# Retention followed by a PReLU feed-forward block: the order of 3802 operations written out in the source instead of found by a list scheduler

## The chip, the cores and the metric

The kernel runs on one core of one Trainium2 chip. The metric is the device time of one execution in microseconds (us). Five engines take part, each working through its own queue in order: TensorE (PE, with PEld for the loading of weights), VectorE (DVE), ScalarE (ACT), GpSimd (POOL) and SyncE (SP), which here issues the DMA transfers.

## The reference

Everything is float32. The first part is retention without softmax, for 8 batches and 8 heads of 576 positions by 64; the second is a feed-forward block on 4608 tokens.

```python
scores = scale * np.matmul(q, k.transpose(0, 1, 3, 2))
Dmat = np.where(rel >= 0, gamma[:, None, None] ** rel[None, :, :], 0.0)
attn = np.matmul(scores * Dmat, v)                 # (8, 8, 576, 64)
x = attn.transpose(0, 2, 1, 3).reshape(4608, 512)
h = x @ w_in                                       # w_in 512 x 2048
g = np.maximum(h, 0.0) + alpha * np.minimum(h, 0.0)
out = g @ w_out                                    # w_out 2048 x 512
```

## The kernel before, in words

Retention is computed in chunks of 64 positions: inside a chunk as masked scores times values, between chunks through a running state (the sums of key times value, decayed from chunk to chunk). The first two batches go in six parts with all heads at once (`load_part`, `part_scale`, `part_transposes`, `part_scores`, `part_states`, `part_values`, `last_part`). The other batches go by pairs of heads in `joint`: per pair one group of score and state products (L920, L923, with one of L913) and two groups of value products (L861). All of these are small matmuls of 64 or 128 rows.

The feed-forward block takes blocks of 256 tokens against an eighth of w_in (256 columns, a "unit") and the matching rows of w_out. While the first two batches run, eight units are computed with plain float32 matmuls (`unit_plain`, L1091; `second_plain`, L1122). All others are computed with operands split into three pieces of float32r, in 128x512 matmuls: h in `unit_roll` (L1188) and `unit_two` (L1222), the second product in `second` (L1340). The pieces of g, of x and of the weights are made by ACT, DVE and POOL (`split_g` L1260 to L1267, `split_roll` L1158 to L1163, `split_w` L783 to L787); w_in and w_out arrive as 64-bit words and are first turned into float32 by two ACT, three DVE and one POOL operation each (`convert`, L730 to L754). At the start and behind the first part, matmuls of the identity whose result nobody reads keep PE occupied (`fill`, L1405).

Every operation is first recorded by `do` (engine, cost, function that issues it, what it reads and writes), in the order of the source, and numbered from 0 to 3801. Nothing is issued then. Afterwards `dues` and `plan` (L229 to L336) order the list: `dues` goes backwards from the end and gives each operation a due time, `plan` goes forwards with constants for an engine's latency, the wire of the DMAs and the loading of instructions and takes the most urgent ready operation. After 12 rounds of that, 243 random changes of the due times in windows of 40 us are tried and kept where the planned total does not get longer. The last loop (L1709 onwards) issues the operations in the planned order. Two things are decided in that loop beside the order in each queue:

- Operations marked `lock` (664 of those of DVE and POOL) never run on both engines at once: where one follows a locked one of the other engine in the order, it waits for it (the dependency with the reason "port").
- In the first 100 us of the plan a DMA issued by SP waits until no more than 5 x 256 KB lie ahead of it (the dependency with the reason "bytes in flight", L211 to L219).

Some lines to which the prediction refers: L455 scales queries or values of a part on POOL, L479 transposes with PE, L485 copies the transposes out with ACT, L503 scores, L510 their mask on DVE, L526 states, L541 their sums on DVE, L574 and L599 values, L588 a copy of two numbers on ACT ("spy") for which the second half of the values waits, L631 the copies of the result into x, L1097 the ReLU of a plain unit.

Of the kernel before, what the change touches and what calls it, by code (L numbers as in the profile page):

```python
# [21 lines left out]
def kernel(  # L22
# [96 lines left out]
    for i in range(NBIT - 1):  # L119
# [8 lines left out]
                            op=ALU.mult)  # L128
# [24 lines left out]
    ops, land = [], [LAND[0]]  # L153
# [65 lines left out]
                flight.append((ins, size))  # L219
        do(eng, 0.56, f, r, w, late=size / rate, hold=hold)  # L220

    flight, now = [], [0.0]
    LIMITED, IN_FLIGHT = 100.0, 5 << 18

    LAT = {"PE": 0.2}

    users = []

    def wait(d, op):  # L229
        return d.land if d.late else 0.0 if d.eng == op.eng else LAT.get(d.eng, 0.1)  # L230

    def dues(after):
        users[:] = [[] for _ in ops]
        for op in ops:
            for d in op.deps:
                users[d.n].append(op)
        due = [0.0] * len(ops)
        left = [len(users[op.n]) for op in ops]
        can = [0.0] * len(ops)
        free = {e: 0.0 for e in BEGIN}  # L240
        ready = {e: [] for e in BEGIN}
        for op in ops:
            if not left[op.n]:
                ready[op.eng].append(op)
        for _ in ops:
            pick = None
            for e, queue in ready.items():
                if queue:
                    t0 = min(max(free[e], can[op.n]) for op in queue)
                    op = max((op for op in queue if max(free[e], can[op.n]) <= t0 + 0.02),  # L250
                             key=lambda op: after[op.n])
                    t = max(free[e], can[op.n])
                    if pick is None or t < pick[0]:
                        pick = t, op
            t, op = pick
            ready[op.eng].remove(op)
            free[op.eng] = t + op.cost
            due[op.n] = -(t + op.cost)
            for d in op.deps:
                left[d.n] -= 1  # L260
                can[d.n] = max(can[d.n], t + op.cost + wait(d, op) + d.late)
                if not left[d.n]:
                    ready[d.eng].append(d)
        return due

    def plan(due):
        last = -min(due)
        left = [len(op.deps) for op in ops]
        ready = {e: [] for e in BEGIN}
        rest = [op.n for op in ops if op.eng == "PE"]  # L270
        end, begin, order = [0.0] * len(ops), [0.0] * len(ops), []
        free, held, port, wire, kinds = dict(BEGIN), {}, [0.0, ""], 0.0, {e: e for e in BEGIN}
        can = [0.0] * len(ops)

        at = [CHUNK - 190, 0.0]
        for op in ops:
            if not op.deps:
                ready[op.eng].append(op)

        def earliest(op):  # L280
            t = max(free[op.eng], can[op.n], op.hold)
            for b in op.banks:
                if b in held:
                    t = max(t, max([x + LAT.get(e, 0.1) for e, x in held[b].items()
                                    if e != op.eng] or [0.0]))
            if op.lock and port[1] != op.eng:
                t = max(t, port[0])
            if op.late:
                t = max(t, wire - BACKLOG, due[op.n] + last - HOLD)
            if op.size and at[0] + op.size > CHUNK:  # L290
                t = max(t, at[1] - op.cost * (CHUNK - at[0]) / op.size)
            return t + SWITCH.get(op.eng, 0.0) * (kinds[op.eng] != op.kind)

        while len(order) < len(ops):
            pick = None
            for e, queue in ready.items():
                if not queue:
                    continue
                c = [(earliest(op), op) for op in queue
                     if e != "PE" or op.n <= rest[0] + AHEAD_PE]  # L300
                if not c:
                    continue
                t0 = min(t for t, _ in c)
                t, op = min((x for x in c if x[0] <= t0 + SLACK.get(e, 0.05)),
                            key=lambda x: (due[x[1].n], x[1].n))
                if pick is None or t < pick[0]:
                    pick = t, op
            t, op = pick
            ready[op.eng].remove(op)
            if op.eng == "PE":  # L310
                rest.remove(op.n)
            begin[op.n] = t
            kinds[op.eng] = op.kind
            free[op.eng] = end[op.n] = t + op.cost
            if op.size:
                at[0] += op.size
                if at[0] >= CHUNK:
                    at[0] -= CHUNK
                    over = end[op.n] - op.cost * at[0] / op.size
                    at[1] = over + FETCH + min(max(wire - over, 0.0), 0.8)  # L320
            if op.late:
                wire = max(wire, t + op.cost) + op.late
                end[op.n] = wire
            for b in op.banks:
                held.setdefault(b, {})[op.eng] = t + op.cost
            if op.lock:
                if port[1] == op.eng or t + op.cost > port[0]:
                    port[:] = [t + op.cost, op.eng]
            order.append(op)
            for u in users[op.n]:  # L330
                left[u.n] -= 1
                can[u.n] = max(can[u.n], end[op.n] + wait(op, u))
                if not left[u.n]:
                    ready[u.eng].append(u)
        total = max(end)
        return total, order, begin, end  # L336

    AHEAD_PE = 150
    WINDOWS, STRETCH, TRIES, ROUNDS = 27, 20.0, 9, 9
    CHUNK, FETCH = 256, 3.1  # L340
    BACKLOG, HOLD = 2.0, 30.0
    LAG, HOLD_X = 2, 100.0
    X_TWO, QUICK, NQUICK, WDVE = 12, 13, 2, 16
    PUMP_R = ((1, 1), (1, 1))
    EARLY, JOINTS = 1, {(s, i): 1 for s in range(14) for i in range(2) if (s, i) not in ((0, 0), (8, 1), (10, 1), (13, 0), (13, 1))}
    PUMP0, PUMP = ((1, 2), (0, 1), (0, 1), (0, 1)), ((1, 2), (1, 2), (0, 1), (0, 1))
    GROUPS = (("v0",), ("v1",), ("x", "su"))
    SLACK, SWITCH = {"PE": 0.2}, {"PE": 0.1}
    BEGIN = {"PE": 1.9, "ACT": 0.5, "DVE": 5.5, "POOL": 5.4, "SP": 0.5}


    def slot(pool, tag, shape, dtype=FP32, bank=False):
        return Slot(tag, lambda: pool.tile(shape, dtype, tag=tag, name=f"{tag}_{next(serial)}"),
                    bank)
# [619 lines left out]
    order = [(kb, (2, 3, 0, 1) if kb % 2 and kb > 1 else (0, 1, 2, 3)) for kb in range(NKB - 2)]  # L974
# [599 lines left out]
    queue = []  # L1574
# [24 lines left out]
    free = [0, 1, 2, 3, 4]  # L1599
# [20 lines left out]
    last = singles - 1  # L1620
    t = 8
    for s in range(last):
        some = [visits[kb] for kb in (1 + s, 2 + s) if 2 <= kb <= last]
# [63 lines left out]
    second_last(*queue)  # L1687


    due = dues([op.n for op in ops])  # L1690
    best = made = plan(due)
    for _ in range(12):
        again = dues(made[3])
        made = plan(again)
        if made[0] < best[0]:
            best, due = made, again
    rng = np.random.RandomState(1)
    for n in range(ROUNDS * WINDOWS):
        lo = STRETCH * (n // TRIES % WINDOWS)
        some = [i for i, t in enumerate(best[2]) if lo <= t < lo + 2 * STRETCH]  # L1700
        other = list(due)
        for i, x in zip(some, rng.uniform(-1, 1, len(some)) * (1.0, 3.0, 9.0)[n % 3]):
            other[i] += x
        made = plan(other)
        if made[0] <= best[0]:
            best, due = made, other

    port = None
    for op in best[1]:  # L1709
        now[0] = best[2][op.n]  # L1710
        ins = op.fn()
        if op.lock:
            if port and port[0] != op.eng:
                tc.add_manual_dep(ins.ins, port[1].ins.name, mybir.DependencyInfo(
                    mybir.DependencyClass.Sync, mybir.DependencyReason.DATA), reason="port")
            port = op.eng, ins
# [31 lines left out]
```

## Time and profile before

| what | value |
|---|---|
| runs | 923.28, 919.66, 919.31 us; median 919.66 us |
| span of the profiled execution, first to last instruction | 917.4 us |
| own time of the profiled execution | only its span is listed; the median is 2.26 us above it |
| PE busy | 906.9 us, 99% of the span |
| DVE, ACT, POOL busy | 60%, 55%, 57% |
| DMA | 121.32 MB, mean 132 GB/s |

Times in the trace are counted from the start of the span. PE's busy time is the union of its matmuls, whose ends are modelled and overlap; how long a stretch of matmuls takes is therefore read from start to start. An idle time is shown with what ended it; "issue" is a wait for nothing that the profile shows. SP's time is that of issuing, not of moving bytes.

### The profile page before, as it was taken

The numbers are of one execution on the slowest core, as the hardware profiler recorded it, in microseconds if no ns is written. First come the engines' busy times: TensorE is split into PE (matmuls) and PEld (weight loads), VectorE is DVE, ScalarE is ACT, GpSimd is POOL, SyncE is SP. The second block draws the span as 40 slices with busy tenths as digits, with TensorE's granted clock in tenths as the row PEclk, the third lists the DMA queues.
The fourth block names the chain that finished last, engine by engine and source line by source line (L and its number), as shares of the span: only waits on it lengthen the run. The fifth ranks groups of instructions, "written<-read, shape, count | busy, mean of one in ns | idle before, by whom it ended". The sixth has DMA issues, their size and how long they took to land. (4 is left out here: it accounts for less than half of the span.)

```text
span 917.4 us, 19097 instructions
## 1 busy us (share of the span) xinstructions
PE 906.9 (99%) x7289; PEld 737.8 (80%) x7289; DVE 548.0 (60%) x1003; ACT 503.9 (55%) x1010; POOL 520.2 (57%) x461
## 2 busy tenths in 40 slices
PE   7999999999999999999999999999999999999998
PEld 6767688887888888888888888888888888888886
DVE  5786766667677667676757776344444534344343
ACT  4575455646565656565746555537463636364441
POOL 4776746456466665674542244665656656574624
PEclk9999999999999999999999999999999999999999
DMA  9995688977988879895243332212121322211112
GB/s 216 251 235 86 164 189 186 198 178 155 221 192 194 209 166 201 193 189 181 93 138 130 102 125 65 86 57 81 58 89 56 99 73 86 74 64 47 47 46 69
DMA packets 235947, 121.32 MB, mean 132 GB/s; under 512 B 203456, under 2 KB 203728, under 8 KB 235856
## 3 DMA queue, kind: packets, MB, share of 16 engines
q1 hardware_dynamic: 235712, 119.98, 52.1%
q8 instruction: 57, 0.93, 0.4%
q14 instruction: 34, 0.28, 0.1%
q10 hardware_dynamic: 144, 0.13, 0.0%
HBM read 74.19 MB, written 32.51 MB: 116 GB/s over the span
## 5 line engine op out<-in xcount | busy, mean ns | idle before, releaser
L1340 PE MATMUL pso<-w,g 128*128 128x512 f32 x1392 | 338.8, 391 | 0.0
L1340 PEld LDWEIGHTS pso<-w,g 128*128 128x128 f32 x1392 | 258.9, 188 | 55.2 <-POOL g L1267 1.2
L1264 POOL TENSOR_TENSOR g<-ga_all,g 128x512 fp32r<-128x512 f32 x76 | 97.9, 1291 | 130.4 <-ACT g L1260 105.0
L1267 POOL TENSOR_TENSOR g<-g 128x512 fp32r<-128x512 f32 x114 | 147.4, 1294 | 23.7 <-DVE su L1066 5.7
L1188 PE MATMUL psh<-lx_x,w 128*128 128x512 f32 (+1 forms) x360 | 86.6, 379 | 0.0
L1188 PE MATMUL psa<-lx_x,w 128*128 128x512 f32 (+1 forms) x360 | 85.4, 376 | 0.0
L1188 PEld LDWEIGHTS psa<-lx_x,w 128*128 128x128 f32 x360 | 65.1, 188 | 13.1 <-issue 0.4
L1188 PEld LDWEIGHTS psh<-lx_x,w 128*128 128x128 f32 x360 | 64.2, 188 | 12.9
L1260 ACT ACTIVATE g<-ga_all 128x512 fp32r<-128x512 f32 x76 | 47.6, 631 | 43.0 <-PE pso L1340 21.0
L1256 POOL TENSOR_TENSOR g<-g 128x512 fp32r<-128x512 f32 x22 | 28.5, 1296 | 64.0 <-DVE g L1253 38.3
L1264 POOL TENSOR_TENSOR g<-vn,g 128x512 fp32r<-128x512 f32 x25 | 32.4, 1297 | 37.5 <-ACT g L1260 34.9
L1340 PE MATMUL pso<-lx_x,g 128*128 128x512 f32 x216 | 53.5, 390 | 0.1
L1163 POOL TENSOR_TENSOR lx_x<-lx_x 128x512 fp32r<-128x512 f32 x28 | 35.9, 1294 | 26.0 <-DVE lx_x L1160 26.0
L941 DVE SCALAR_TENSOR_TENSOR at<-psa,pf,mask 64x512 f32<-64x512 f32 x48 | 36.0, 749 | 21.1 <-PE psh L861 10.2
L1340 PEld LDWEIGHTS pso<-lx_x,g 128*128 128x128 f32 x216 | 40.4, 188 | 9.0 <-DVE o L1363 0.7
L1262 ACT ACTIVATE g<-ga_all 128x512 fp32r<-128x512 f32 x76 | 47.2, 621 | 0.0
L1358 DVE TENSOR_TENSOR op<-pso,op 128x512 f32<-128x512 f32 x35 | 24.0, 686 | 31.3 <-PE pso L1340 31.2
L1202 ACT COPY ga_all<-psh 128x512 f32<-128x512 f32 (+1 forms) x30 | 16.7, 558 | 39.1 <-PE psh L1188 37.4
L861 PEld LDWEIGHTS psh<-at,vn 128*64 128x64 f32 x864 | 27.9, 137 | 8.7 <-issue 3.6
L1222 PE MATMUL psh<-w,w 128*128 128x512 f32 x144 | 34.6, 389 | 0.0
L1222 PE MATMUL psa<-w,w 128*128 128x512 f32 x144 | 34.6, 389 | 0.0
L754 POOL TENSOR_TENSOR wa<-wa,op 128x512 int32<-128x512 int32 x16 | 21.0, 1311 | 23.1 <-DVE wa L751 19.1
(329 smaller groups left out, 1883.3 us busy)
## 6 DMA issues: line engine op xcount, KB each, us to landing
xk<-x SPq DMA_DIRECT2D x18, 512.0 KB, 3.7
ok<-o SPq DMA_DIRECT2D x36, 256.0 KB, 2.9
op<-ok SPq DMA_DIRECT2D x18, 512.0 KB, 3.9
out_dram<-o SPq DMA_DIRECT2D x35, 256.0 KB, 2.3
x<-xk SPq DMA_DIRECT2D x16, 512.0 KB, 5.6
qx<-in_q_dram SPq DMA_DIRECT2D x96, 72.0 KB, 3.4
kx<-in_k_dram SPq DMA_DIRECT2D x96, 72.0 KB, 3.3
kn<-in_k_dram SPq DMA_DIRECT2D x48, 144.0 KB, 3.4
```

The lines of the kernel that those rows point to most:

```text
L861: nc.tensor.matmul(pv[i].get()[half(h2), (j - js[0]) * C:(j - js[0] + 1) * C], vns[n % 2][:, h2, j], mt.get()[:, h2, j], start=True, stop= ...
L941: nc.vector.scalar_tensor_tensor(out=mt.get()[half(1 - h2), h2, j], in0=fro[x], scalar=pf[x, 1, h:h + 1], in1=mask[x, None, :].to_broadcas ...
L1163: do("POOL", 1.29, lambda h=h, l=l, d=d: nc.gpsimd.tensor_tensor(out=piece(d()), in0=h(), in1=l(), op=ALU.subtract), [(g, 0, n), (g, 1, n) ...
L1188: nc.tensor.matmul(out_of(p), w[:, c0:c0 + P], xp(l, cc), start=(l != 1 and cc == 0), stop=(l > 0 and cc == NCC - 1))
L1222: nc.tensor.matmul(p.get(), w[:, c0:c0 + P], piece(words_of(g)[:, o:o + DM]), start=(l != 1 and cc == 0), stop=(l > 0 and cc == NCC - 1))
L1256: do("POOL", 1.29, lambda: nc.gpsimd.tensor_tensor(out=piece(to.get()[:, 2]), in0=to.get()[:, 0], in1=to.get()[:, 1], op=ALU.subtract), [( ...
L1260: do("ACT", 0.64, lambda: nc.scalar.mul(piece(to.get()[:, 2]), whole(), BELOW), both, [(to, 2)])
L1262: do("ACT", 0.64, lambda: nc.scalar.mul(piece(to.get()[:, 0]), whole(), BELOW * 2.0 ** -12), both, [(to, 0)])
L1264: do("POOL", 1.29, lambda: nc.gpsimd.tensor_tensor(out=piece(to.get()[:, 1]), in0=whole(), in1=to.get()[:, 2], op=ALU.subtract), both + [( ...
L1267: do("POOL", 1.29, lambda: nc.gpsimd.tensor_tensor(out=piece(to.get()[:, 2]), in0=to.get()[:, 0], in1=to.get()[:, 1], op=ALU.subtract), [( ...
L1340: nc.tensor.matmul(a[2 * m + b].get(), piece(g.get()[:, l, f, m * P:(m + 1) * P]), w_piece(u, 2 + f, l), start=(cell["first"] and f == 0 a ...
L1358: do("DVE", 0.69, lambda: nc.vector.tensor_tensor(out=t(), in0=p1.get(), in1=t(), op=ALU.subtract), [(p1, 0)], [tk])
```

## The change

`dues`, `plan`, their constants and the search over due times are removed. In their place stands `ORDER`, a string with the numbers of all 3802 operations, and the loop issues them in this order. The recorded operations, their functions and their dependencies are the same. The limit on bytes in flight holds for the first 453 entries of the order; before, it held for the 442 operations planned to begin before 100 us.

```diff
-    flight, now = [], [0.0]
-    LIMITED, IN_FLIGHT = 100.0, 5 << 18
...
-    def dues(after):
...
-    def plan(due):
...
+    flight, now = [], [0]
+    LIMITED, IN_FLIGHT = 453, 5 << 18
...
-    due = dues([op.n for op in ops])
-    best = made = plan(due)
...
-        made = plan(other)
-        if made[0] <= best[0]:
-            best, due = made, other
+    ORDER = (
+        "0 6-7 11 53 2 1 3 71 4 75 13 5 16 12 17 76 8-10 14 74 15 22 19 18 77 47 20 103 25 21 72 55 23-24 104 "
+        "33 73 105 48-49 32 50-52 101 54 102 56 78 106-107 57 108 58 40 26 79 27 60 28 109 29 62 34 30 36 110 "
+        "63 31 145 59 37-38 130 61 35 129 85 127 131 41 80 132 42 86 128 133-134 93 43-44 39 94 45 135 46 157 "
...
+    )
+    order = []
+    for run in ORDER.split():
+        a, _, b = run.partition("-")
+        order += range(int(a), int(b or a) + 1)
+    assert sorted(order) == list(range(len(ops)))
...
-    for op in best[1]:
-        now[0] = best[2][op.n]
+    for now[0], n in enumerate(order):
+        op = ops[n]
         ins = op.fn()
```

Set beside the order that the planner found, queue by queue, the two differ only up to about 470 us of the trace; from there on each engine has the same sequence. In the differing stretch 256 of PE's 764 operations stand in another place (by at most 10 places), 418 of ACT's 1010 (at most 24), 440 of DVE's 963 (at most 37), 152 of POOL's 446 (at most 14) and 451 of SP's 619 (at most 58).

More of the change, by code (lines that the diff above doesn't have):

```diff
@@ L220, in dma @@
         do(eng, 0.56, f, r, w, late=size / rate, hold=hold)
-    flight, now = [], [0.0]
-    LIMITED, IN_FLIGHT = 100.0, 5 << 18
[L225 to L230, printed above, removed]
-    def dues(after):
[L233 to L264, printed above, removed]
@@ L266, in plan @@
-    def plan(due):
[L267 to L341, printed above, removed]
+    flight, now = [], [0]
+    LIMITED, IN_FLIGHT = 453, 5 << 18
     LAG, HOLD_X = 2, 100.0
@@ L347 @@
     GROUPS = (("v0",), ("v1",), ("x", "su"))
-    SLACK, SWITCH = {"PE": 0.2}, {"PE": 0.1}
-    BEGIN = {"PE": 1.9, "ACT": 0.5, "DVE": 5.5, "POOL": 5.4, "SP": 0.5}
     def slot(pool, tag, shape, dtype=FP32, bank=False):
@@ L1687 @@
     second_last(*queue)
-    due = dues([op.n for op in ops])
-    best = made = plan(due)
[L1692 to L1703, printed above, removed]
-        made = plan(other)
-        if made[0] <= best[0]:
-            best, due = made, other
+    ORDER = (
[176 rows of a table added]
+    )
[4 more added lines that the diff above has]
+    assert sorted(order) == list(range(len(ops)))
     port = None
-    for op in best[1]:
-        now[0] = best[2][op.n]
+    for now[0], n in enumerate(order):
+        op = ops[n]
         ins = op.fn()
```

173 rows, old and new, of the table ORDER are left out of this document.

## The prediction

> **What bounds the kernel now.** I read the page first, then the busy time by stages, then PE's waits stage by stage, and at last the sequence of single instructions where a wait stands.
>
> ```profile
> span 917.4 us, 19097 instructions
> ...
> PE 906.9 (99%) x7289; PEld 737.8 (80%) x7289; DVE 548.0 (60%) x1003; ACT 503.9 (55%) x1010; POOL 520.2 (57%) x461
> ...
> PEclk9999999999999999999999999999999999999999
> ...
> q8 instruction: 57, 0.93, 0.4%
> ```
>
> ```profile
> 0.00:40.00 40.00, 33.76 (x674) 26.94 (x675) 27.97 (x79) 19.97 (x34) 23.52 (x35) 1.00 0.98 226
> 40.00:460.00 420.00, 419.73 (x4602) 336.03 (x4601) 294.23 (x557) 252.59 (x524) 253.85 (x207) 1.00 0.79 180
> 460.00:900.00 440.00, 440.00 (x1957) 364.48 (x1956) 217.77 (x356) 229.90 (x450) 237.88 (x216) 1.00 0.25 79
> ```
>
> The second fence gives, for three stretches, the busy time of PE, PEld, DVE, ACT and POOL, then the granted clock, the DMA share and GB/s. From 40 us on PE is never idle: 419.73 of 420.00 and 440.00 of 440.00. The clock is granted in full. The order differs only up to about 470 us, and an order changes no matmul. So it can win only two things: PE's idle time in the first 40 us (6.24 us, DMA share 0.98), and time that hides in the busy 420 us because matmuls there follow each other less densely than they could. Here is the whole of PE's idle time by what ended it, first up to 40 us, then (last row) from 40 to 460 us:
>
> ```profile
> PE psh L1405 <- POOL ident masks.py:199: 1.7, 1, 1.7
> PE pso L574 <- issue: 1.3, 1, 1.3
> PE pso L479 <- POOL w L455: 1.1, 2, 0.7
> PE psa L599 <- ACT spy L588: 1.0, 1, 1.0
> PE psh L1091 <- POOL lx_w L754: 0.4, 1, 0.4
> PE pso L574 <- DVE g L510: 0.3, 1, 0.3
> PE psh L599 <- issue: 0.3, 1, 0.3
> ...
> PE psh L861 <- DMA vn<-su: 0.2, 1, 0.2
> ```
>
> The first row, 1.7 us, is the constant table that PE's first instruction needs; it stands ahead of all ordered operations and stays. What the order can touch is 4.4 us before 40 us and 0.2 us after.
>
> **The change, part by part.** The sum is made against the span of 917.4 us. The profiled execution's own time isn't listed beside it; I take the distance to the median of the runs, 919.66 - 917.4 = 2.26 us, as fixed.
>
> ```profile
> 6.99 2.15 POOL L455 TENSOR_TENSOR w<-w,tp 128x512 f32<-128x512 f32 x2 [3.88 <-DMA w<-in_q_dram]
> 17.78 0.69 ACT L730 ACTIVATE ga_all<-lx_w 128x512 f32<-128x512 f32 x1
> 18.97 2.61 PE L1405 MATMUL psh<-ident 128*128 128x128 f32 x20
> 19.97 0.69 DVE L751 SCALAR_TENSOR_TENSOR lx_w<-lx_w,psa 128x512 int32<-128x512 int32 x1
> 20.75 1.04 POOL L455 TENSOR_TENSOR w<-w,tp 128x512 f32<-128x512 f32 x1 [2.87 <-DMA w<-in_v_dram]
> 20.83 0.68 ACT L732 ACTIVATE lx_w<-lx_w 128x512 int32<-128x512 uint32 x1
> 20.98 0.70 DVE L740 TENSOR_SCALAR psa<-ga_all 128x512 f32<-128x512 f32 x1 [0.33 <-ACT ga_all L730]
> 21.54 0.58 ACT L631 COPY x<-pso 64x512 f32<-64x512 f32 x1
> 21.75 1.30 POOL L754 TENSOR_TENSOR lx_w<-lx_w 128x512 int32<-128x512 int32 x1
> 23.11 1.99 PE L1091 MATMUL psh<-x,lx_w 128*128 128x256 f32 x8 [0.43 <-POOL lx_w L754]
> ```
>
> 1. The first loads (SP) and transposes (PE). SP issues both halves of the queries ahead of the second half of the keys, so the scaling at 6.99, which waited 3.88 us for them, begins earlier; PE takes the transposes in the order in which they become ready, and a transpose of the next part moves from behind to ahead of the values (L574). This attacks 1.1 + 0.3 us and part of the 1.3 us. I cost it at nothing: behind it stand ten filler matmuls (20 rows, 2.61 us at 18.97) that count for no result, and the plain unit at 23.11 that waits for weights. The first thirteen transfers, both halves of the first weights among the last of them, are the same set in both orders, so the weights don't land sooner. If this cover were gone, up to 1.4 us would be won.
>
> 2. The first weights. ACT's second operation on them moves from 20.83 to directly behind the first (17.78), and POOL adds (21.75) before it scales (20.75) instead of after. The add then needs only DVE's result of 19.97 + 0.69 = 20.66 and could run 1.05 us earlier. PE's plain unit also needs the copy of x that ends at 21.54 + 0.58 = 22.12, so it can begin at about 22.2 instead of 23.11: 0.9 us, of which 0.43 us is the visible wait and the rest asks that PE itself arrives sooner (step 1). What is late next is DVE: from 20.98 on its queue runs almost without a gap to the sums that PE's values need, and only its 0.33 us gap goes. I take 0.4 us; ends 0 and 0.9.
>
> 3. The spy copy.
>
> ```profile
> 26.12 1.99 PE L1091 MATMUL psh<-x,lx_w 128*128 128x256 f32 x8
> 28.68 0.68 ACT L730 ACTIVATE w<-w 128x512 f32<-128x512 f32 x1 [1.20 <-DMA w<-in_moe_w_in_dram]
> 29.27 0.58 ACT L1097 ACTIVATE ga_all<-psh 128x512 f32<-128x512 f32 x1
> 29.75 0.68 ACT L732 ACTIVATE w<-w 128x512 int32<-128x512 uint32 x1
> 30.29 0.13 ACT L588 COPY spy<-psh 1x2 f32<-1x2 f32 x1
> 30.49 0.27 PE L599 MATMUL psa<-w,w 64*64 64x64 f32 x2 [1.03 <-ACT spy L588]
> ```
>
> The copy for which PE waits 1.03 us stands on ACT behind two weight operations and a ReLU whose matmuls ended at 26.12 + 1.99 = 28.11. After the change the order is ReLU, spy, weights. PE stopped at 30.49 - 1.03 = 29.46, so the copy can run about 29.5 to 29.65 and PE go on at 29.7: 0.8 us. [...] So I book 0.4 us of the 0.8; ends 0 and 1.03. What is queued behind the copy on ACT, the weight operations, becomes 0.1 us later.
>
> [...]
>
> 4. Changes between kinds of matmul, 40 to 470 us.
>
> ```profile
> 140.17 0.92 PE L861 MATMUL psh<-at,vn 128*64 128x64 f32 x24
> 141.02 1.20 PE L1340 MATMUL pso<-w,g 128*128 128x512 f32 x4
> 142.15 0.57 PE L861 MATMUL psh<-at,vn 128*64 128x64 f32 x12
> 142.64 1.65 PE L1340 MATMUL pso<-w,g 128*128 128x512 f32 x6
> ...
> 140.65 1.29 POOL L1267 TENSOR_TENSOR g<-g 128x512 fp32r<-128x512 f32 x1
> ```
>
> Start to start, the four large matmuls at 141.02 take 142.15 - 141.02 = 1.13 us; undisturbed, one takes 440.00 / 1957 = 0.225 us, four 0.90. Standing between two small groups costs 0.23 us. The twelve small ones take 0.49 us against half of 141.02 - 140.17 = 0.85, that is 0.43: 0.06 us. One such excursion costs 0.29 us, inside "busy" time. In the order of before PE goes from small matmuls to the split ones 30 times and back 29 times; in the new order 25 and 24 times (the place shown is one: the three small groups there become neighbours). 5 x 0.29 = 1.45 us. Against it, one plain unit (L1122) now stands apart from its neighbour, between split matmuls: one more excursion, at the price of the same row 0.29 us. 1.2 us remain; ends 0 (merged groups that wait for each other's operands) and 1.45.
>
> 5. The wait of 0.2 us for a DMA at L861: two groups of values change places, so the wait has cover. 0.2 us; ends 0 and 0.2.
>
> 6. All other moves (DVE 440, ACT 418, SP 451, POOL 152 places) touch engines that are not on the path. Their cover is their idle time from 40 to 460 us: 420 - 294.23 = 126 us on DVE, 166 on POOL. I cost them at nothing, though not safely: the nearest row to a limit is POOL's plane at 140.65, ready at 141.94, of which PE makes use at 142.64. Its slack is 0.70 us, and a 1.29 us operation put ahead of it would be felt by 0.6 us. What hides SP's moves is DMA's share falling to 0.79 after 40 us; before that it is full, and a load moved ahead delays those behind it by its own bytes.
>
> Sum: 0.4 + 0.4 + 1.2 + 0.2 = 2.2 us; 917.4 - 2.2 = 915.2 us of span, 919.66 - 2.2 = 917.5 us of device time, 0.24% less. 0.5% of the median, 4.6 us, is about what a measurement of this kernel can tell from no change, so this counts as the same.
>
> **The rivals.**
>
> A. The hand-overs between DVE and POOL decide, and the kernel gets slower. Locked operations of the two never overlap, and each change of engine in the order is a wait. Counted in the two orders, these changes rise from 88 to 104 in the differing stretch. The price of each is at most the POOL operation of 1.29 us that the other side must sit out. If half of the 16 reach PE in full, 8 x 1.29 = 10.3 us come and 2.2 go: 927.8 us. It outweighs the gain and shows as slower from six of them (7.7 - 2.2 = 5.5 us). For it speaks the slack of 0.70 us above. Against it speaks that the 88 of before cost PE nothing: 0.2 us of idle time from 40 to 460 us, and that for a DMA.
>
> [...]
>
> B. More is won. Were all of the 4.4 us of waits before 40 us to go, with 1.45 us of excursions and 0.2, the time would be 919.66 - 6.05 = 913.6 us. It asks that loads and weight conversion in the first 40 us have room; DMA's share of 0.98 and DVE's near gapless queue speak against it.
>
> C. The moves change nothing that counts: the early lead is spent waiting for the next load, and merged small groups wait for each other. 919.5 us. For it speaks that loads fill the first 40 us and that the first weights have the same set of them ahead.
>
> **How the numbers follow.** Chances: the forecast 0.5 (its own range 916 to 919), C 0.22, B 0.15, A 0.13. The predicted time is the forecast's, 917.5 us. The range has to leave out no more than 2 in 10: it reaches to 913.2, just past B, and upwards to 922.5, which is C with two of the hand-overs of A felt (919.5 + 2 x 1.29 = 922.1), and leaves out most of A. Faster by over 0.5% means under 915.06 us: B and a little of the forecast's edge, 0.16. Slower by over 0.5% is A, 0.13. The rest, 0.71, is the same.
>
> **What would show it.** Right: PE's idle time in the first 40 us falls by about 1 us; the row "L599 <- ACT spy" falls under 0.3 us while "issue" waits grow; L1091's wait for L754 is gone; from 40 to 460 us PE stays idle under 0.5 us, and the first matmul of the stage that is the same in both kernels comes about 2 us sooner. Wrong: new waits of PE for POOL L1267 or L1264 between 40 and 470 us (A); a first plain unit that begins at 21 us or sooner (B); or the common stage beginning at the same time as before (C).

## The result and the profile after

The changed kernel takes 915.87 us (median of 6 runs, 915.15 to 917.96), the kernel before beside it 919.48 us (917.42 to 923.28). The ratio is 0.9963 [0.9948, 0.9979]: 3.6 us less, a gain that is real but under half a per cent. A later set of 12 runs gave 916.54 us and 0.9966 [0.9954, 0.9979].

Of the profiled execution (span 915.0 us, own time 916.74 us), the head of the page, then the busy time of PE, PEld, DVE, ACT and POOL by stage, with the granted clock, DMA share and GB/s behind them, then PE's waits up to 40 us:

```profile
span 915.0 us, 19113 instructions
...
PE 905.5 (99%) x7289; PEld 738.2 (81%) x7289; DVE 552.0 (60%) x1003; ACT 503.2 (55%) x1010; POOL 519.8 (57%) x461
```

```profile
0.00:40.00 40.00, 34.45 (x675) 27.63 (x676) 29.43 (x80) 19.57 (x33) 22.56 (x35) 0.96 1.00 227
40.00:460.00 420.00, 420.00 (x4619) 338.24 (x4618) 297.34 (x557) 252.65 (x526) 257.76 (x211) 1.00 0.78 181
460.00:900.00 440.00, 439.89 (x1949) 363.59 (x1948) 219.17 (x357) 230.18 (x450) 236.89 (x215) 1.00 0.24 79
```

```profile
PE psa L358 <- DVE w L420: 1.9, 1, 1.9
PE psh L1284 <- POOL ident masks.py:199: 1.7, 1, 1.7
PE pso L358 <- DMA w<-in_k_dram: 0.5, 1, 0.5
PE pso L405 <- POOL w L334: 0.4, 2, 0.2
PE pso L1001 <- DVE ga_all L981: 0.3, 1, 0.3
PE pso L382 <- ACT w L364: 0.2, 1, 0.2
PE psa L478 <- ACT spy L467: 0.2, 1, 0.2
```

Lines behind the removed block carry numbers lower by 121: L358 is the L479 of before (transposes), L478 its L599, L467 its L588, L740 its L861, L1219 its L1340.

PE's idle time up to 40 us fell only from 6.24 to 5.55 us. The waits that the prediction wanted to shorten are gone or smaller, but a new one of 1.9 us stands in front of them, and the granted clock, 1.00 before, is 0.96 on average here. From 40 to 460 us the last 0.27 us of idle is gone and the stretch holds 4619 matmuls against 4602.

How far ahead is the new kernel? I set the start of each operation of PE in one trace against its start in the other, wherever both had done the same set of operations. The lead is 1.17 us at 9 us, then turns to -1.38 us at 20 us (behind the new wait and the slow clock), +0.12 at 32 us, 0.42 at 100 us, 2.48 at 438 us, and 2.42 us at the end. So in these two executions the start gave next to nothing and the stretch from 40 to 460 us gave about 2.2 us. (Other executions of the same two orders divide the gain otherwise; the experiments come back to that.) The second part comes in steps at the places that the prediction counted in its step 4. The first of them, where before had 24 small matmuls, four large, 12 small, in the changed kernel:

```profile
138.67 1.27 PE L740 MATMUL psh<-at,vn 128*64 128x64 f32 x36
...
141.06 3.04 PE L1219 MATMUL pso<-w,g 128*128 128x512 f32 x12
```

The 36 small ones now run as one, and the lead grows by 0.35 us there, by 0.50 us at 221 (where the profile of before has its DMA wait), 0.20 at 225, 0.23 at 241, 0.33 at 341 to 345 and 0.36 us at 356 to 367. (The execution of the later set, which has no dip of the clock, gives these same steps within 0.05 us.)

### The profile page after: what moved, and what is told of

Read it like the earlier page. It is cut to its first block, busy times and chain, and to the rows that moved or that the text cites. A ratio compares the mean times of both kernels' runs of the same rounds, so it can differ in the third digit from the quotient of the medians.

```text
span 915.0 us, 19113 instructions
## 1 busy us (share of the span) xinstructions
PE 905.5 (99%) x7289; PEld 738.2 (81%) x7289; DVE 552.0 (60%) x1003; ACT 503.2 (55%) x1010; POOL 519.8 (57%) x461
## 5 line engine op out<-in xcount | busy, mean ns | idle before, releaser
L1219 PE MATMUL pso<-w,g 128*128 128x512 f32 x1392 | 338.4, 392 | 0.0
L1219 PEld LDWEIGHTS pso<-w,g 128*128 128x128 f32 x1392 | 259.0, 188 | 55.2 <-POOL g L1146 0.9
L1219 PE MATMUL pso<-lx_x,g 128*128 128x512 f32 x216 | 53.5, 390 | 0.1
L1219 PEld LDWEIGHTS pso<-lx_x,g 128*128 128x128 f32 x216 | 40.4, 188 | 9.0 <-DVE o L1242 0.7
L740 PEld LDWEIGHTS psh<-at,vn 128*64 128x64 f32 x864 | 27.4, 138 | 8.7 <-issue 6.1
L712 POOL TENSOR_TENSOR qx<-qx,tabx 128x576 f32<-128x576 f32 x24 | 27.6, 1149 | 9.0 <-DMA qx<-in_q_dram 7.4
```

What stands on the lines that cost most here:

```text
L712: return nc.gpsimd.tensor_tensor(out=qh, in0=qh, in1=tabx[:, None, c, :, None].to_broadcast([P, NJ, 2, 32]), op=ALU.mult)
L740: nc.tensor.matmul(pv[i].get()[half(h2), (j - js[0]) * C:(j - js[0] + 1) * C], vns[n % 2][:, h2, j], mt.get()[:, h2, j], start=True, stop= ...
L1219: nc.tensor.matmul(a[2 * m + b].get(), piece(g.get()[:, l, f, m * P:(m + 1) * P]), w_piece(u, 2 + f, l), start=(cell["first"] and f == 0 a ...
```

## The experiments

All are written as an `ORDER` in the form of the changed kernel. Times are medians of 6 to 12 runs. The kernel before, run beside them in three sets, had 919.12, 919.32 and 919.41 us.

**The form alone.** Before's order, as its planner puts it out, written out:

```diff
-        "0 6-7 11 53 2 1 3 71 4 75 13 5 16 12 17 76 8-10 14 74 15 22 19 18 77 47 20 103 25 21 72 55 23-24 104 "
...
+        "0 3 2 6 1 4 7 11 8 5 53 9 71 13 10 74 76 16 12 17 24 14 22 19 15 75 23 18 47 77 21 48 20 72 25 49 55 "
...
```

> The order that the kernel before's scheduler puts out, written out in the source in the form of the changed kernel; nothing else differs from before. The theory, that only the order of the operations acts on the time: the ratio to before is 1.000 within 0.002. The rival, that the form (no scheduler, no search, one source line for all of it) acts as well: the ratio is 0.996, as with the change itself.

Measured: 919.03 us, 0.9995 [0.9979, 1.0011]. The form does nothing that this interval could show, and the rival's 0.996 lies outside it: it is the order that acts. Its profile (waits up to 40 us, then the window 16.6 to 20.0 us) taught something else:

```profile
PE pso L453 <- issue: 1.9, 1, 1.9
...
PE psa L478 <- ACT spy L467: 0.2, 1, 0.2
```

```profile
16.60:20.00 3.40, 3.40 (x104) 3.00 (x102) 0.75 (x2) 2.22 (x4) 1.35 (x2) 0.53 1.00 230
```

The order of before, too, can run into half a clock at 17 us. In this execution PE comes late to the values of the second part, and the wait for the spy copy, 1.0 us in the profile that the prediction used, is 0.2 us. That 1.0 us was no fixed cost of the order. Nor was the DMA wait at L861: this execution has no wait of PE at all from 40 to 900 us, and it makes up 0.47 us on the profile of before at that place, with the order unchanged.

That profile was also not the usual case in its clock. One stretch of 3.41 us at half clock, the length in the profile of the changed kernel, takes 0.0019 off a mean over 917 us, so a run whose mean clock is 0.998 or less has lost at least about one such stretch, wherever it lay. Of the 96 runs of before in the three sets 68 have such a mean clock, of the 18 runs of the changed kernel 7. So the half clock is no mark of the changed order; it is the profile with which the prediction worked that lacks it.

Set against this execution, which goes to half clock at 16.8 us as the changed kernel does at 16.7 us, the changed kernel leads by 0.93 us at 40 us and by 2.45 us at the end: 0.9 us from the start and 1.5 us behind it, where the pair above gave 0.15 and 2.3.

**A cut at 99 us**, where PE's own sequences meet but those of the other engines don't. The first 454 entries come in before's order, then every other operation in the changed one (the counterpart has 448 in the changed order ahead):

```diff
-        "0 6-7 11 53 2 1 3 71 4 75 13 5 16 12 17 76 8-10 14 74 15 22 19 18 77 47 20 103 25 21 72 55 23-24 104 "
+        "0 3 2 6 1 4 7 11 8 5 53 9 71 13 10 74 76 16 12 17 24 14 22 19 15 75 23 18 47 77 21 48 20 72 25 49 55 "
...
```

> The first 454 operations, to the place that PE reaches at 99 us, in before's order, and all behind them in the changed order. The theory, from the leads of the two traces (0.34 us at 99 us, 2.42 at the end), is that the gain lies behind the start: 2.1 us under before, a ratio of 0.9977. The rival, by the prediction's terms (0.8 us at the start, 1.4 behind): 1.4 us under before, 0.9985. A second rival, that the start's gain is as large as its new wait of 1.9 us allows where the clock does not fall, and the rest small: within 0.8 us of before.

> The counterpart: the first 448 operations in the changed order, all behind them in before's. The theory, that the start holds a new wait of 1.9 us for a load and, in executions like the profiled one, 3.4 us at half clock behind it: 0.3 us under before where the clock falls, up to 1.9 us under where it doesn't, so a ratio between 0.998 and 1.000, with two groups of times. By the prediction's terms: 0.8 us under, 0.9991, in one group. PE's idle before the transposes of the first part should be 1.9 us again.

Measured: 924.07 us, 1.0046 [1.0029, 1.0063], and the counterpart 924.70 us, 1.0055 [1.0036, 1.0074]. Both miss every theory; the wait of 1.9 us that was expected in the counterpart is 0.5 us there. The waits of PE at the cut, first kernel and counterpart, and the first one's busy time in the windows behind its wait:

```profile
PE psh L740 <- ACT x L759: 3.9, 1, 3.9
```

```profile
PE psh L740 <- issue: 4.7, 1, 4.7
```

```profile
106.10:112.90 6.80, 6.03 (x33) 3.88 (x34) 4.37 (x11) 2.07 (x6) 1.49 (x2) 0.50 0.58 122
113.00:116.40 3.40, 3.40 (x23) 2.83 (x23) 0.75 (x2) 1.73 (x5) 0.79 (x1) 1.00 0.76 231
```

The seam itself costs 3.9 and 4.7 us of idle, and 6.8 us at half clock follow. Behind the seam the first kernel wins 1.55 us against the written-out order of before (lead -6.42 us at 107 us, -4.87 at 438), close to the 1.5 us of the changed kernel against the same execution. As a test of the split these two are inconclusive; what they show is that halves of two orders don't fit each other where one engine has run ahead.

**A cut at 36 us**, at a place where on each of the five queues the set of operations ahead is the same in both orders: 33 operations of PE, 30 of ACT, 34 of DVE, 17 of POOL and 32 of SP. They come in before's sequence, the others in the changed one (and the other way round in the counterpart).

```diff
-        "0 6-7 11 53 2 1 3 71 4 75 13 5 16 12 17 76 8-10 14 74 15 22 19 18 77 47 20 103 25 21 72 55 23-24 104 "
+        "0 3 2 6 1 4 7 11 8 5 53 9 71 13 10 74 76 16 12 17 24 14 22 19 15 75 23 18 47 77 21 48 20 72 25 49 55 "
...
```

> Before's order on each engine up to 36 us, at a place where all five queues have the same operations behind them in both orders; the changed order from there on. From the leads of the two profiled executions (0.15 us at 36 us, 2.42 at the end), the gain lies behind the start: 2.2 us under before, a ratio of 0.9976. By the prediction's terms (0.8 in the start, 1.4 behind it): 1.4 under, 0.9985. If the seam itself is what costs, as in the cut at 99 us, PE waits at it for over 1 us and the time is above before's.

> The counterpart of the seam at 36 us: the changed order before it, before's order behind it. That seam with before's start had a median 2.1 us under before, which leaves 1.35 us of the changed kernel's 3.45 for the start. If the two add up, this is 1.35 us under before, a ratio of 0.9985; by the leads of the two profiled executions, of which only the changed one had the dip, 0.2 us under, 0.9998.

Measured: before's start with the changed rest 917.22 us, 0.9978 [0.9966, 0.9991]; the changed start with before's rest 919.20 us, 0.9989 [0.9971, 1.0006]. There is no wait at the seam. By the medians the rest is worth 2.1 us (0.8 to 3.1 by its interval), and the start alone 0.2 us, not told from nothing (its interval reaches to 2.7). The two sum to 2.3 us, the whole change to 2.9 and 3.6 us in its two sets.

The profiled executions allow a wider look at the start. Six of them have before's order up to 40 us, five the changed one (the seam at 36 us counts for the order ahead of it). Against the profile of before, the six stand at 40 us between -0.77 and 0.09 us, on average at -0.35; the five stand between -0.78 and 1.22, on average at 0.38. So the start may well be worth about 0.7 us, but executions of one and the same start lie up to 2.0 us apart, and what it is worth, alone or with its own continuation, is left open.

**A cut at 136 us** in the same way (128 operations of PE, 147 of ACT, 172 of DVE, 72 of POOL and 135 of SP in before's sequence, the others in the changed one).

> The same with the seam at 136 us: before's order up to there, the changed order behind it. The leads of the two profiled executions say 0.35 us at 136 us and 2.42 at the end, so 2.1 us are left: a ratio of 0.9977. If the gain came from how the loads and filters stood at 40 to 136 us, it would be lost: within 0.5 us of before, 0.9995 or more.

Measured: 918.08 us, 0.9985 [0.9969, 1.0001], so 1.24 us under before. Its one profiled execution has a lead over before of 0.30 us at 99 us and 2.38 us at 427 us, which is the theory's 2.1; the median says less, and the interval takes in 2.1 us and nothing as well. Against the written-out order of before the same execution gains 1.5 us behind 99 us (0.86 there, 2.39 at 389). Where between 36 and 460 us the gain stands is shown by the traces, not by these medians.

**Joining on PE alone**, against the written-out order of before. On PE a small group moves ahead of the large ones that parted it from its like: 712 ahead of 698, 1170 of 1220, 1242 of 1240, 1813 and 1812 of 1797, 1896 of 1882. The other four queues stay. The first of the five in the string:

```diff
-        "711 725 696 673 708 726 698 674 714 749 709 734 712 752 735 697 721 715 710 702 727 719 699 722 703 "
+        "711 725 696 673 708 726 674 714 749 709 734 712 698 752 735 697 721 715 710 702 727 719 699 722 703 "
...
```

> Before's order, with only PE's operations moved at the five places where the change joins two groups of small matmuls; the orders of ACT, DVE, POOL and SP are before's. The prediction's step 4 prices an excursion at 0.29 us: 5 x 0.29 = 1.45 us under before, a ratio of 0.9984, and 0.34 us more (0.9980) if the wait for a load at 219 us goes with it. The rival, that the moved groups then wait for their inputs or hold up the softmax behind them, gives 0 to 0.5 us under before, with waits of PE at those five places in the trace.

Measured: 918.84 us, 0.9995 [0.9979, 1.0010]: the median is the rival's, though the interval takes in the theory's 0.9984 as well. The traces decide: against the written-out order of before the lead is 0.38 us ahead of the first place and 0.50 behind the last, so the five joins brought 0.1 us. The first joined place wins 0.35 us, the third 0.25 and the fifth 0.34, close to the price of 0.29; but at the second PE then waits, and 0.35 us more are lost at 149 us, among matmuls that are called busy:

```profile
222.77 0.33 PE L792 MATMUL psh<-qT,kT 64*64 64x64 f32 x4 [0.47 <-ACT x L759]
```

The copy of x by ACT for which PE waits in this row stands where the old order wanted it.

**Splitting on PE alone**, the opposite, from the changed kernel (29 places of PE's sequence differ):

```diff
-        "667 685 691 675 637 670 692 669 693 711 694-695 714 749 712 672-673 713 715 750 671 674 752 703 677 "
...
+        "667 685 691 675 637 670 692 669 693-695 672-673 713 711 714 749 715 750 671 674 752 677 698 712 723 "
...
```

> The changed kernel with PE's order at the five places where it joins two groups of small matmuls put back to before's; the other queues keep the changed order. By the price of step 4 (0.29 us each), 1.45 us are lost: a ratio to before of 0.9978, where the changed kernel had 0.9963, and five more crossings of 0.25 to 0.35 us each in the trace. The rival: as with the joins made on PE alone, which were paid back in waits, the loss here is half or less, 0.9971 or below, or it is larger, with waits of PE at the places, since the softmax behind each is ordered for the joined group.

Measured: 927.36 us, 1.0078 [1.0056, 1.0100], 10.8 us above the changed kernel of the same set. PE's waits from 100 to 460 us, then two groups at the first place:

```profile
PE psh L1067 <- ACT x L759: 3.3, 4, 1.8
PE pso L1219 <- POOL g L1146: 1.4, 1, 1.4
PE pso L1219 <- DVE o L1242: 0.6, 1, 0.6
```

```profile
143.24 0.57 PE L740 MATMUL psh<-at,vn 128*64 128x64 f32 x12
145.23 2.11 PE L1219 MATMUL pso<-w,g 128*128 128x512 f32 x8 [1.42 <-POOL g L1146]
```

By the price of 0.29 us it should have lost 1.45 us; the rival that had it larger, with waits of PE, came. PE asks for pieces of g and for free buffers in an order that POOL and ACT no longer follow. From 136 to 460 us PE is idle for 6.0 us (busy 318.01 of the 324 us); and 1.5 us of its lag behind the second profile of the changed kernel stand ahead of the first changed place, where the two have the same order. How the rest divides I did not take apart.

**Keeping PE busy through the new wait.** Filler matmuls of the identity go where PE idles at 13.3 us in the changed kernel, 14 and then 6 of them. The new operation, 63, stands behind 48 in the order, and the numbers of all later ones shift by one:

```diff
     fill(10, 0.25, of_pe())
+    fill(14, 0.25)
```

> The changed kernel with one more group of 14 filler matmuls on PE, between the states of the first part and the transposes of the second, where its trace shows PE idle from 13.27 to 15.17 us, with the granted clock at 0.5 for 3.41 us behind. [...] Rival: the drop doesn't come from the idle, or the wait grows by the fillers; 915.9 or more, with the clock at 0.5 as before.

> The filler group between the states of the first part and the transposes of the second with 6 matmuls instead of 14: a group of 14 took 3.39 us in its trace, 0.24 us each, so 6 take 1.45 us of the 1.9 us that PE idles there and end before the load lands. Theory: the clock stays at 1.0 in nearly all runs and nothing is overshot; 915.2 us, the changed kernel's runs without the dip, a ratio to before of 0.9955. [...]

Measured: 917.44 us, 0.9979 [0.9966, 0.9992] with 14, and 916.61 us, 0.9967 [0.9952, 0.9983] with 6. With both the clock stayed: 11 of 12 runs of each had a granted clock of 0.999 or 1.0, and both profiles show 1.00 up to 40 us. The time did not fall below the changed kernel's. With 14 (a filler is two matmuls, 3.39 / 14 = 0.24 us) the group outlasts the wait by 1.3 us (its rows, then PE's waits up to 60 us):

```profile
13.23 3.39 PE L1284 MATMUL psh<-ident 128*128 128x128 f32 x28
16.46 0.60 PE L358 MATMUL psa<-ident,w 128*128 128x128 f32 x4
```

```profile
PE psh L453 <- issue: 0.8, 1, 0.8
...
PE pso L494 <- issue: 0.6, 1, 0.6
```

The first row stands at 55.4 us, where the changed kernel has no wait; the lead over it falls by 0.99 us there. The profile names no releaser for either of the two waits, so what they come from is not shown. With 6 the group fits, the clock stays, and the median is that of the changed kernel all the same (916.54 in that set).

**Taking the wait away.** The K load of the second part (74) goes back ahead of its Q load (76):

```diff
-        "0 6-7 11 53 2 1 3 71 4 75 13 5 16 12 17 76 8-10 14 74 15 22 19 18 77 47 20 103 25 21 72 55 23-24 104 "
+        "0 6-7 11 53 2 1 3 71 4 75 13 5 16 12 17 74 76 8-10 14-15 22 19 18 77 47 20 103 25 21 72 55 23-24 104 "
```

> The changed kernel with one DMA moved: the K load of the second part goes ahead of its Q load in SP's queue, as it did before the change. Theory: the transposes that waited 1.9 us for it start about 1.2 us sooner, the clock does not fall, and the start gives the 0.8 us that the prediction had for it: 914.9, a ratio of 0.9953. Rival: the Q load is then as late as the K load was, and PE waits as long for the transposes of the Q rows one operation on: no change, 915.9.

Measured: 915.30 us, 0.9956 [0.9940, 0.9972], with 9 of 12 runs between 914.94 and 915.63 us and 11 of 12 with a mean clock of 0.999 or 1.0. PE in the two kernels, the changed one first:

```profile
12.58 0.69 PE L405 MATMUL pso<-w,w 64*64 64x64 f32 x32 [0.21 <-POOL w L334]
15.17 0.63 PE L358 MATMUL psa<-ident,w 128*128 128x128 f32 x4 [1.90 <-DVE w L420]
...
16.57 1.03 PE L358 MATMUL psa<-ident,w 128*128 128x128 f32 x4
17.52 2.25 PE L494 MATMUL pso<-g,w 64*32 64x64 f32 x96
19.70 0.81 PE L358 MATMUL psh<-ident,w 128*128 128x128 f32 x4
20.35 0.83 PE L1284 MATMUL psh<-ident 128*128 128x128 f32 x6
```

```profile
13.14 0.66 PE L358 MATMUL psa<-ident,w 128*128 128x128 f32 x4
...
14.97 0.45 PE L453 MATMUL pso<-g,w 64*64 64x64 f32 x11 [0.68 <-issue]
15.97 0.66 PE L358 MATMUL psa<-ident,w 128*128 128x128 f32 x4 [0.56 <-POOL w L334]
16.56 1.40 PE L494 MATMUL pso<-g,w 64*32 64x64 f32 x96
17.88 0.66 PE L358 MATMUL psh<-ident,w 128*128 128x128 f32 x4
18.38 2.40 PE L1284 MATMUL psh<-ident 128*128 128x128 f32 x20
```

The transposes begin 2.03 us sooner, and of that 1.97 us are left at the fillers. The row of 1.90 us names DVE as the releaser, but it was the load: moving nothing but that load takes the wait away. The length of that wait is not fixed, though. In the five profiled executions that have the changed order here it is 1.90, 1.99, 0.66, 0.54 and 0.19 us, and only the two long ones are followed by half clock; the ones of 0.66 and 0.19 us name the load as the releaser. The Q rows wait 0.56 us in exchange, so a quarter to a third of the rival is there. At the end 1.46 us of the lead over the profiled changed kernel remain. The median is the lowest of all kernels here, but its interval overlaps that of the changed kernel, and the two did not run side by side.

**The changed kernel again.**

> The changed kernel once more, unaltered, beside the runs of the next three. Of its six first runs three had a granted clock of 0.999 to 1.0 and 915.2 us, three one of 0.998 and 916.5 to 918.0. If the dip of the clock at 16.6 us is what parts them, the two groups come again, 1.3 to 2.8 us apart, around a median of 915.9; if it was chance, one group, and no tie of time to clock.

Measured: 916.54 us, 0.9966 [0.9954, 0.9979]. The two groups do not come again: the eight runs with a clock of 0.999 or 1.0 took 915.2 to 917.6 us (median 916.6), the four with 0.997 and 0.998 took 916.1 to 918.4 (median 916.5). The profiled execution had no dip and the clock at 1.00 up to 40 us, led the first profile by 1.82 us at 20 us, by 1.07 at 36 us, and by 0.27 us at 99 us, with PE's waits from 40 to 136 us among what took it back:

```profile
PE psh L792 <- DVE qT L718: 0.3, 1, 0.3
PE psh L358 <- ACT w L364: 0.2, 1, 0.2
```

So here the dip does not by itself part short runs from long ones. In the kernel before it goes with the time: in its three sets the runs with a clock of 0.999 or 1.0 have medians of 917.9, 918.5 and 918.6 us, the others 919.8, 919.3 and 920.2. What sets the 3 us between runs of one kernel is not settled.

## Why the prediction held, step by step

The time (917.5 us forecast, 915.9 and 916.5 measured) lies in the range, and the gain stays under 0.5% as forecast. But the sum came out near for reasons that only in part are those of its steps. 0.8 us were booked for the start and 1.4 behind it. The cut at 36 us gives 0.2 and 2.1 us by its medians, the changed kernel against the profile of before 0.15 and 2.3, against the written-out order 0.9 and 1.5. So the gain behind the start is shown, with 1.5 to 2.3 us the size of step 4 or somewhat more; how much the start gives is not. Two of the terms, in steps 3 and 5, priced waits that before's order does not have in another execution.

1. First loads and transposes, booked at 0. Wrong in its reason: the step reckoned what could be won behind the cover of the fillers, not what could be lost ahead of them. I had looked at the loads of the weights, "the same set in both orders", and not at which transposes wait for the load that now stands behind another. In the first profile of the changed kernel the 1.9 us of idle and the clock behind it ate the 1.17 us of lead that the earlier transposes had brought. Before's order has its own wait of 1.9 us and its own half clock there in the written-out execution, and against that one 0.3 us remain at the fillers.
2. First weights, 0.4 us. Held: the wait of the plain unit for the POOL add (L1091 for L754 in before) is gone, and from the fillers to that unit the lead grows by 0.5 us against the profile of before and by 0.56 against the written-out order. 0.3 us of the wait reappears one unit on, at L1001, in the first profile of the changed kernel, and not in the second. (The 1.05 us by which the add could run earlier are 21.75 - 20.66 = 1.09; nothing hangs on it.)
3. Spy copy, 0.4 of 0.8 us. No run shows the 0.4: that half of the 0.8 would be lost again behind the copy was my estimate. What the runs showed in its place is a wait of 0.2 us, as was named for the whole 0.8, and no "issue" row that grew behind it. But the step took a cost of one execution for a cost of the order: with before's own order written out the wait is 0.2 us too, in an execution where PE comes later. At this copy the changed kernel gains 0.79 us on the profile of before, and the written-out order gains the same 0.79 us on it.
4. Fewer changes between kinds of matmul, 1.2 us. The size held: the steps of the lead at the five places, without the 0.50 us at 221 that the written-out order makes up as well, sum to 0.35 + 0.20 + 0.23 + 0.33 + 0.36 = 1.5 us against 5 x 0.29 = 1.45. Of the excursion to be subtracted, 0.12 us was seen. What failed is its claim to stand alone: joined on PE alone the places gain 0.1 us in the trace and nothing that the medians show.
5. The DMA wait at L861, 0.2 us. The wait is gone, but the reason is not shown: it is gone as well with before's own order written out. This too was a cost of one execution.
6. All other moves, 0. Wrong as a reason, and harmless for the sum: a gain of their own is not seen, but without the moves on ACT, DVE, POOL and SP step 4 pays its gain back.

Of the rivals, A (DVE and POOL hand-overs) did not come: PE waits for nothing from 40 to 460 us though the changes of engine rose from 88 to 104. B was not reached; 915.3 us, with the load moved, is the nearest. C describes the start against the profile of before, and only that.

What the prediction left out altogether is the granted clock: it said "The clock is granted in full" of before and took that as given for what comes after. It had read a view of one execution, and that view counts as full what it has no record of. In the trace of before the first record of the clock is at 7.30 us. Ahead of it ten filler matmuls take almost as long as the twenty at 18.97 us, which take 2.61:

```profile
1.69 2.50 PE L1405 MATMUL psh<-ident 128*128 128x128 f32 x10 [1.69 <-POOL ident masks.py:199]
```

The distance of 2.26 us between span and time, taken as fixed, is 1.7 to 2.1 us in the other profiled executions; the forecast, a difference from the median, does not use it.

## What to carry to other kernels

When single moves have tuned an order, the joint gain belongs to the set: price a move on the bounding engine together with the moves that bring its operands and free its buffers, and test it so too, or a good price turns into waits. Where loads fill a stage, ask of each load that goes back one place which operation of the bounding engine waits for it. And a wait of one execution is not a cost of the order until a second execution of the same order shows it.

## What the runs showed of the hardware

The granted clock fell in seven of the 14 profiled executions within the first 40 us: its mean there is 0.96 in these and 1.00 in the other seven. Each of the first seven has a wait of PE of 1.6 to 2.2 us in that time; six of the others have none above 1.3 us, beside the 1.7 us that PE's first instruction waits in every one. The seventh, with the splitting on PE alone, waits 2.2 us at one place and keeps 1.00, so the length of a single wait does not tell the two kinds apart; what does is not shown. Five executions at the same place:

| execution | PE idle, 12.9 to 16.4 us | granted clock, 16.6 to 20.0 us |
|---|---|---|
| before's order written out | 1.93 us | 0.53 |
| changed kernel, first profile | 1.90 us | 0.51 |
| changed kernel, second profile | 1.35 us | 1.00 |
| before | 1.33 us | 1.00 |
| load moved | 1.24 us | 1.00 |

The ends of matmuls are modelled, and with them these idle times. In the first profile of the changed kernel the clock is at 1.00 from 6.41 to 16.65 us, at 0.50 for the next 3.41 us, and at 1.00 again behind them. With before's order up to 99 us PE was idle for 3.09 of the 3.40 us from 102.7 us on; from 106.1 to 112.9 us the clock was 0.50, and 1.00 from 113.0 to 116.4 us. The price of the slow stretch is read from the rows of the changed kernel and of the one with the load moved: the same three groups take 20.35 - 16.57 = 3.78 us in the one and 18.38 - 15.97 = 2.41 us in the other, 1.4 us.

The waits called "issue" at the first small matmuls are 1.3 and 0.3 us in the profile of before, none in the first profile of the changed kernel, 0.7 us in its second, 1.9 us with before's order written out. They move with the execution by up to 1.9 us, more than half of the whole gain of the change, so none of these single figures should be taken for the price of an order.
